# Last batch of an attention and expert layer: key sums and nine query transposes of a pair in one step, ten steps instead of twelve

## The chip, the cores and the metric

The kernel runs on one core of one Trainium2 chip. The metric is the device time of one execution in microseconds (us). Before the change it is 881.54 us, the median of three runs (880.99 to 881.73).

The core has five engines with a queue each, and each works its queue in order. PE does matrix products and transposes, and writes to PSUM (eight banks). ACT, DVE and POOL do element by element work; ACT and DVE read PSUM. SP issues most transfers.

## What is computed

Linear attention with random features for 4 batches of 8 heads (576 positions of 64 elements), then four experts on every position, each a product, a relu and a second product, weighted and summed:

```python
def phi(x):
    h = einsum('bhsd,md->bhsm', x, omega) - sum(x * x, -1) / 2
    return exp(h - max(h, -1)) / sqrt(m)
q_p, k_p = phi(q * D**-0.25), phi(k * D**-0.25)
kv, z = einsum('bhsm,bhsd->bhmd', k_p, v), sum(k_p, 2)
x = einsum('bhsm,bhmd->bhsd', q_p, kv) / (einsum('bhsm,bhm->bhs', q_p, z) + 1e-6)
...
for e in range(E):
    out += p[:, e:e + 1] * (relu(x @ w1[e]) @ w2[e])
```

The kernel splits an operand of a large product into a high and a low part of a faster number format (names that end in `h` and `l`) and adds three products, high by high, low by high and high by low.

## The kernel before, in words

The 2304 positions pass the experts in three blocks. Each block takes eight **visits**, one for half of the hidden units of an expert. The change concerns the second block, 768 positions, whose visits are numbered 1 to 8 here. They lie at 283.3, 316.0, 356.0, 392.7, 428.9, 466.6, 502.8 and 535.5 us of the profiled execution, and the last ends at 566.5 us.

While PE computes this block, the last batch's attention is worked in between. It has four **pairs** of heads, called pair 1 to 4 here. `later_ticks` (L469) is a generator that yields after each **step** of a pair, and `emit` (L1383) calls it at fixed points of the visits. Nothing reorders the work afterwards (`manual_schedule`), so every engine's queue is the order in which this code runs.

A visit is written by `fast` (L895). First come fourteen products of six matmuls each, seven for each of two groups of hidden units (`product`, L929; their matmuls are L937), and three half tiles of the second product (`begun`, L1006). Then come the rest of six output tiles (`outputs`, L751, its matmuls L756 to L758). A half tile is six matmuls. Where the first yield of a visit stands, after the products and the half tiles, is **slot 0**; slots 1 to 6 stand after output tiles 0 to 5. Slot 6 is the last before the next visit's products.

Four parts of a visit matter here:

- **Product 1 is copied before product 6.** Product 1 goes to a bank, ACT copies it to SBUF (`keep`, L941, its copy is L943), and product 6 adds to the same bank. Products 2 and 5 lie between. So PE reaches product 6 after eighteen matmuls, and waits there if the copy isn't done. Further on, the sums of `both` (L947, DVE, L951) free the banks of product 2 and 5.
- **The next visit's weights** are made in slices, one call of the generator `sides` (L675) after the products and after each output tile. After tile 1 DVE does four additions in place (L687 to L690) on the first half of the weights, after tile 2 ACT makes the high part (`w1sh`, L567) and POOL the low part (`w1sl`, L570). After tiles 3 and 4 the same comes for the second half. The additions write what the two others read.
- **The output tile** is weighted and added to `acc` by DVE (`gather`, L785), in visit 1 written by ACT (L783).
- **The stores of the weights** (`keep_sides`, L666) go over SP's queue ahead of later loads.

A pair's twelve steps, with the engines that they occupy:

1. keys projected on PE (L266, L277), their maxima on DVE (L282, L287), and the bias of the exponential on DVE (`bias`, L289: two small operations on 128 x 9 elements, L292 and L293, each with both inputs in SBUF)
2. the exponentials of the keys' tails and of the first half (ACT, L306 and L299), and the queries' squared lengths (DVE, L255)
3. the exponentials of the keys' second half (ACT, L299)
4. to 6. the same for the queries; steps 5 and 6 load the next pair's keys and queries
7. `sum_keys` (L309): eighteen matmuls on PE, evicted by ACT and DVE (L319, L320); the next pair's v is loaded and its keys are squared on POOL (L251)
8. `turn(0)` (L322): four transposes on PE, evicted by ACT and DVE (L338, L339)
9. `turn(1)`: five transposes (L328, L332), evicted likewise; the next pair's queries are squared on POOL
10. `numerators(0)` (L344): six matmuls, evicted by ACT (L365, L366); the next pair's lengths of the keys (L255, DVE)
11. `invert(0)` (DVE, L371), `times(0)` (POOL, L376), `numerators(1)`
12. `invert(1)`, `times(1)`

Six steps of `opening` (L378) come first: loads, squares on POOL and lengths of the first pair. That makes 54 steps.

How many steps a slot gets is set by a rate in `windows` (L1386): 54 steps over 0.8 of the 56 slots of the block, 1.205 a slot. After n slots all steps whose number is below 1.205 n have been written.

Of the kernel before, what the change touches and what calls it, by code (L numbers as in the profile page):

```python
# [14 lines left out]
def attention_moe(ctx, tc, kT, qT, kd, qd, kn, qn, vn, omT, probs, w1, w2, out):  # L15
# [11 lines left out]
    _, NP, D, _ = kT.shape  # L27
# [3 lines left out]
    E, FP, P, _ = w1.shape  # L31
# [69 lines left out]
    NV = len(HALVES)  # L101
# [276 lines left out]
    def opening(p, both=False):  # L378

        p.load("k")  # L380
        yield
        p.load("q")
        yield
        p.load_v()
        p.load_tails()
        yield
        p.square("k")
        yield
        p.square("q")
        yield  # L390
        p.lengths("k")
        if both:
            p.lengths("q")
        yield

    def joint_ticks(pairs):

        before = None
        for p, then in zip(pairs, pairs[1:] + [None]):
            p.project("k")  # L400
            p.project_tails("k")
            p.project("q")
            p.project_tails("q", beside="k")
            p.maxima("k")
            p.maxima_tails("k")
            p.bias("k")
            yield
            p.exp_tails("k")
            p.exp("k", 0)
            p.maxima("q")  # L410
            p.maxima_tails("q")
            p.bias("q")
            yield
            p.exp("k", 1)
            if then:
                then.load("k")
            yield
            if before:
                before.numerators(0)
            if then:  # L420
                then.load("q")
            yield
            p.exp_tails("q")
            p.exp("q", 0)
            if before:
                before.invert(0)
            if then:
                then.square("k")
            yield
            if before:  # L430
                before.numerators(1)
                before.times(0)
            if then:
                then.lengths("k")
                then.square("q")
            yield
            p.exp("q", 1)
            if before:
                before.invert(1)
            yield  # L440
            if before:
                before.times(1)
            if then:
                then.lengths("q")
            yield
            p.sum_keys()
            p.turn(0)
            p.turn(1)
            if then:
                then.load_v()  # L450
                if then.hp == 0:
                    then.load_tails()
            before = p
            yield
        yield from divided(before)
# [13 lines left out]
    def later_ticks(pairs):  # L469

        for p, then in zip(pairs, pairs[1:] + [None]):
            p.project("k")
            p.project_tails("k")
            p.maxima("k")
            p.maxima_tails("k")
            p.bias("k")
            yield
            p.exp_tails("k")
            p.exp("k", 0)
            p.lengths("q")  # L480
            yield
            p.exp("k", 1)
            yield
            p.project("q")
            p.project_tails("q")
            p.maxima("q")
            p.maxima_tails("q")
            p.bias("q")
            yield
            p.exp_tails("q")  # L490
            p.exp("q", 0)
            if then:
                then.load("k")
            yield
            p.exp("q", 1)
            if then:
                then.load("q")
            yield
            p.sum_keys()
            if then:  # L500
                then.load_v()
                then.square("k")
            yield
            p.turn(0)
            yield
            p.turn(1)
            if then:
                then.square("q")
            yield
            p.numerators(0)  # L510
            if then:
                then.lengths("k")
            yield
            p.invert(0)
            p.times(0)
            p.numerators(1)
            yield
            p.invert(1)
            p.times(1)
            yield  # L520
# [4 lines left out]
    BIG = {1: (START, 6 * P), 2: (START + 6 * P, 8 * P)}  # L525
# [5 lines left out]
    N0 = len(visits)  # L531
# [274 lines left out]
    def plain(v):  # L806
        n = visits[v][4]
        last = v == N0 - 1
        ready = sides(v + 1) if last else iter(())
        hs = []  # L810
        for f in range(FH):
            ps = bank("g1")
            hidden(v, f, n, ps, range(2))
            if n > 2 * P:
                yield 0.5
            hidden(v, f, n, ps, range(2, NP))
            hs.append(relu(ps, n))
            split_w()
            if f != 1:
                next(ready, None)  # L820
            if last and f:
                next(building, None)
            yield 0.5
        tiles = n // P
        for t in range(tiles):
            ps = bank("g2")
            outputs(v, hs, ps, t, range(2))
            if v == N0 - 2 and t in (0, 2):
                next(building)
            if last:  # L830
                next(building, None)
            yield 0.5
            outputs(v, hs, ps, t, range(2, FH))
            gather(v, ps, t)
            gathered(v, t)
            for _ in range(FH // tiles):
                split_w()
            next(ready, None)
            if last:
                next(building, None)  # L840
            yield 0.5
# [477 lines left out]
    def first_visit(g1):  # L1319
        hs = [relu(ps, 2 * P) for ps in g1[:2]]  # L1320
        yield 0.5
        for ps in g1[2:]:
            split_w(lo=nc.vector)
            hs.append(relu(ps, 2 * P))
            yield 0.5
        split_w(lo=nc.vector)
        split_w(lo=nc.vector)
        yield 0.5
        for t in range(2):
            ps = bank("g2")  # L1330
            outputs(0, hs, ps, t, range(FH))
            gather(0, ps, t)
            gathered(0, t)
            split_w()
            split_w(lo=nc.vector)
            yield 1

    def first_rest(pairs, then):

        def ahead(hp):  # L1340
            if hp < NP:
                pairs[hp].project("q", 1)
                pairs[hp].project("q", 2)

        def exps(hp):
            if hp < NP:
                pairs[hp].exp("q", 1)
                pairs[hp].exp("q", 2)

        ahead(0)  # L1350
        pairs[2].square("q1", nc.gpsimd)
        yield
        exps(0)
        ahead(1)
        pairs[3].square("q1", nc.gpsimd)
        yield
        for hp, p in enumerate(pairs):
            if hp:
                pairs[hp - 1].finish(1)
            p.turn(1, nc.vector)  # L1360
            p.turn(2, nc.vector)
            if hp == 0:
                nc.vector.tensor_scalar(om_r, om_r, QS, None, ALU.mult)
            if hp:
                next(then, None)
            yield
            exps(hp + 1)
            ahead(hp + 2)
            if hp:
                next(then, None)  # L1370
            yield
            p.numerators(1)
            yield
        pairs[-1].finish(1)
        yield

    def chain(*many):
        for x in many:
            yield from x
# [3 lines left out]
    def emit():  # L1383
        pairs, g1 = begin()
        later = [Halves(b, hp) for b in range(1, B) for hp in range(NP)]
        windows = {  # L1386
            0: (first_rest(pairs, opening(later[0], both=True)), 15 / 11),
            3: (joint_ticks(later[:-NP]), 76 / 45.4),
            N0: (chain(opening(later[-NP]), later_ticks(later[-NP:])), 54 / (NV * (BIG[1][1] // P + 1) * 0.8)),
        }  # L1390
        ticks, n, done, per = iter(()), 0, 0.0, 0
        for v in range(len(visits)):
            if v in windows:
                for _ in ticks:
                    pass
                ticks, per = windows[v]
                n, done = 0, 0.0
            for share in first_visit(g1) if v == 0 else fast(v) if v >= N0 else plain(v):
                done += share
                while n < done * per:  # L1400
                    next(ticks, None)
                    n += 1
        store(0)

    with tc.manual_schedule():
        emit()
# [58 lines left out]
```

## Time and profile before

| what | us |
|---|---|
| median of three runs | 881.54 |
| profiled execution | 883.9 |
| its span, first to last instruction | 882.1 |
| PE busy | 874.8 |
| DVE, POOL, ACT busy | 573.6, 553.1, 467.4 |

The profiled execution took 2.4 us longer than the median of the runs. PE has a matmul under way in 99% of the span, at the full granted clock in every slice of the page, so what the other engines do matters where PE has to wait for it. All times that follow are us from the start of the span. In a timeline a row is the start, the duration, the engine, the line, the operation and its tiles; an `x2` merges equal ones that follow each other; what stands in brackets is the engine's idle time before it and what ended that. Matmuls overlap, so their pace is read from their starts.

### The profile page before, as it was taken

To read this page: it belongs to the slowest core of one execution; us is meant where nothing else is said; L and a number is where in the kernel's file an instruction comes from. 1 tells how busy PE (TensorE), PEld (TensorE's weight loads), DVE (VectorE), ACT (ScalarE), POOL (GpSimd) and SP (SyncE) were. 2 spreads that over 40 slices of the span, in tenths; PEclk is the share of its full clock that TensorE was granted. 3 is DMA by queue.
4 is the path that set the end of the run, shared out by engine and by line. 5 is a ranking of instruction groups with operands and counts; after the bars stand their busy time and mean duration, and the time that the engine had idled before them with its cause. 6 is when DMAs were issued, how large, how long until landed. Compare 5 with 4: busy or idle time off the path is not lost.

```text
span 882.1 us, 14766 instructions
## 1 busy us (share of the span) xinstructions
PE 874.8 (99%) x5484; PEld 787.5 (89%) x5484; DVE 573.6 (65%) x1025; ACT 467.4 (53%) x1039; POOL 553.1 (63%) x494
## 2 busy tenths in 40 slices
PE   9999999999999989999999999999999999999998
PEld 9888898989888988989889899899989898998988
DVE  6755566666667556575756756965748476574847
ACT  6564687776774554556545554544443434444342
POOL 6656465555644454354444446779898887979874
PEclk9999999999999999999999999999999999999999
DMA  7565355444521847446274354645152442415132
GB/s 183 167 214 170 111 162 177 129 137 138 186 63 58 286 125 276 174 148 246 74 279 164 123 215 164 235 152 158 57 179 81 141 161 85 156 60 180 53 116 96
DMA packets 64296, 134.01 MB, mean 152 GB/s; under 512 B 10368, under 2 KB 20800, under 8 KB 64224
## 3 DMA queue, kind: packets, MB, share of 16 engines
q1 hardware_dynamic: 54256, 102.95, 35.9%
q0 software_dynamic: 9360, 29.82, 10.4%
q8 instruction: 43, 0.70, 0.3%
q10 hardware_dynamic: 608, 0.30, 0.1%
q14 instruction: 29, 0.24, 0.1%
HBM read 98.96 MB, written 34.08 MB: 151 GB/s over the span
## 4 chain that ended last, share of the span: by engine, by line
PE 97%; DVE 2%; DMA 1%; ACT 0%; issue 0%; POOL 0%; SPq 0%; POOLq 0%
PE g L937 30%; PE g L1015 18%; PE g L756 8%; PE g L758 8%; PE g L757 8%; PE g L741 3%; PE g L742 3%; PE g L743 3%; PE kv L317 2%; PE k_ps L266 1%; PE q_ps L266 1%; PE qt_ps L328 1%; PE k_ps L147 1%; PE kv L177 1%; PE nd L207 1%; PE nd L358 1%
## 5 line engine op out<-in xcount | busy, mean ns | idle before, releaser
L785 DVE SCALAR_TENSOR_TENSOR acc<-g,pr,acc 128x256 f32<-128x256 f32 (+1 forms) x278 | 140.2, 542 | 41.6 <-PE g L758 26.1
L570 POOL TENSOR_TENSOR w2l<-w2r,w2h 128x512 fp32r<-128x512 f32 x61 | 79.3, 1308 | 78.7 <-ACT w2h L567 67.3
L570 POOL TENSOR_TENSOR w1sl<-w1r,w1sh 128x512 fp32r<-128x512 f32 (+1 forms) x43 | 75.2, 1749 | 65.2 <-ACT w1sh L567 59.7
L756 PE MATMUL g<-w2h,hh 128*128 128x512 f32 x280 | 111.7, 399 | 0.0
L758 PE MATMUL g<-w2h,hl 128*128 128x512 f32 x280 | 109.6, 391 | 0.0
L757 PE MATMUL g<-w2l,hh 128*128 128x512 f32 x280 | 109.5, 391 | 0.0
L937 PE MATMUL g<-xbh,w1sh 128*128 128x384 f32 (+1 forms) x256 | 93.1, 364 | 2.3 <-ACT sum L943 2.3
L937 PE MATMUL g<-xbl,w1sh 128*128 128x384 f32 (+1 forms) x256 | 92.9, 363 | 0.0
L937 PE MATMUL g<-xbh,w1sl 128*128 128x384 f32 (+1 forms) x256 | 92.6, 362 | 0.0
L943 ACT ACTIVATE sum<-g 128x384 f32<-128x384 f32 (+1 forms) x96 | 52.2, 544 | 69.6 <-PE g L937 68.8
L570 POOL TENSOR_TENSOR w1al<-w1r,w1ah 128x512 fp32r<-128x512 f32 (+1 forms) x45 | 49.6, 1118 | 57.5 <-ACT w1ah L567 51.9
L937 PE MATMUL g<-xbh,w1ah 128*128 128x384 f32 (+1 forms) x192 | 69.9, 364 | 0.0
L937 PE MATMUL g<-xbl,w1ah 128*128 128x384 f32 (+1 forms) x192 | 69.6, 362 | 0.0
L937 PE MATMUL g<-xbh,w1al 128*128 128x384 f32 (+1 forms) x192 | 69.5, 362 | 0.0
L951 DVE TENSOR_TENSOR sum<-g,sum 128x384 f32<-128x384 f32 (+1 forms) x64 | 37.4, 588 | 44.3 <-PE g L937 38.7
L758 PEld LDWEIGHTS g<-w2h,hl 128*128 128x128 f32 x280 | 52.5, 188 | 11.4
L756 PEld LDWEIGHTS g<-w2h,hh 128*128 128x128 f32 x280 | 52.7, 188 | 10.1
L757 PEld LDWEIGHTS g<-w2l,hh 128*128 128x128 f32 x280 | 52.6, 188 | 9.0
L937 PEld LDWEIGHTS g<-xbh,w1sh 128*128 128x128 f32 x256 | 48.1, 188 | 8.3 <-ACT sum L943 2.6
L937 PEld LDWEIGHTS g<-xbl,w1sh 128*128 128x128 f32 x256 | 48.1, 188 | 5.2
L937 PEld LDWEIGHTS g<-xbh,w1sl 128*128 128x128 f32 x256 | 48.1, 188 | 5.1
L961 ACT ACTIVATE hh<-sum 128x384 fp32r<-128x384 f32 x48 | 25.1, 525 | 50.8 <-DVE sum L951 50.4
(220 smaller groups left out, 2472.2 us busy)
## 6 DMA issues: line engine op xcount, KB each, us to landing
w1r<-in_w SPq DMA_DIRECT2D x54, 512.0 KB, 3.7
w2r<-in_w SPq DMA_DIRECT2D x76, 256.0 KB, 3.1
kept<-w1sh SPq DMA_DIRECT2D x16, 512.0 KB, 5.3
kept<-w1sl SPq DMA_DIRECT2D x16, 512.0 KB, 5.5
w1sh<-kept POOLq DMA_DIRECT2D x16, 512.0 KB, 4.9
w1sl<-kept POOLq DMA_DIRECT2D x16, 512.0 KB, 5.6
kept<-w1ah SPq DMA_DIRECT2D x16, 384.0 KB, 4.9
kept<-w1al SPq DMA_DIRECT2D x16, 384.0 KB, 5.0
```

The costliest lines, as they stand in the source:

```text
L570: lo.tensor_tensor(c, t, f32(a), ALU.subtract)
L741: nc.tensor.matmul(ps[:, :n], a[:, w], hi, start=(hp == 0), stop=False)
L742: nc.tensor.matmul(ps[:, :n], a[:, w], lo, start=False, stop=False)
L743: nc.tensor.matmul(ps[:, :n], r[:, w], hi, start=False, stop=(hp == NP - 1))
L756: nc.tensor.matmul(ps, ha[:, ts_], wa, start=(c == 0), stop=False)
L757: nc.tensor.matmul(ps, ha[:, ts_], wc, start=False, stop=False)
L758: nc.tensor.matmul(ps, hc[:, ts_], wa, start=False, stop=(c == FH - 1))
L785: nc.vector.scalar_tensor_tensor(to, ps, sc, to, ALU.mult, ALU.add)
L937: nc.tensor.matmul(ps, a[:, w], x[:, k], start=(start and k + at == 0), stop=(k == 1 and at == 2), skip_group_check=not start)
L943: nc.scalar.activation(t, P_[g][where], AF.Copy)
L951: nc.vector.tensor_tensor(t, P_[g][where], kept, ALU.add)
L1015: nc.tensor.matmul(to, x, w, start=(start and f + k == 0), stop=(f + k == 3), skip_group_check=not start)
```

## The change

Step 7 now holds `sum_keys`, `turn(0)` and `turn(1)`: eighteen matmuls and nine transposes, with all their evictions, and the load and the square that step 7 had. The old step 8 is gone. What step 9 had besides, the square of the next pair's queries, goes to the front of `numerators(0)`. A pair has ten steps, the stage 46, and the rate is 46 over the same slots, 1.027 a slot.

```diff
             p.sum_keys()
+            p.turn(0)
+            p.turn(1)
             if then:
                 then.load_v()
                 then.square("k")
             yield
-            p.turn(0)
-            yield
-            p.turn(1)
             if then:
                 then.square("q")
-            yield
             p.numerators(0)
...
-            N0: (chain(opening(later[-NP]), later_ticks(later[-NP:])), 54 / (NV * (BIG[1][1] // P + 1) * 0.8)),
+            N0: (chain(opening(later[-NP]), later_ticks(later[-NP:])), 46 / (NV * (BIG[1][1] // P + 1) * 0.8)),
```

With the rate, other steps move too. Before, about every fifth slot got two steps; now nearly every slot gets one. Counted out from the two rates, the slots that the prediction speaks of (K for keys, Q for queries; project, first and second exponentials as E1 and E2):

| visit, slots | before | now |
|---|---|---|
| 1, slots 4, 5, 6 | pair 1: lengths and K project; K E1; K E2 | lengths; K project; K E1 |
| 2, slots 3, 4, 5, 6 | turn(0); turn(1); numerators(0); numerators(1) | Q E2; sum and turns; numerators(0); numerators(1) |
| 3, slots 3, 4, 5, 6 | pair 2: Q project; Q E1; Q E2 and sum; turn(0) | K E2; Q project; Q E1; Q E2 |
| 4, slots 0, 1, 2, 3 | pair 2: turn(1); numerators(0); numerators(1); invert(1) and, of pair 3, K project | sum and turns; numerators(0); numerators(1); invert(1) |
| 4, slots 4, 5, 6 | pair 3: K E1; K E2; Q project | K project; K E1; K E2 |
| 5, slot 6 | pair 3: invert(1), and K project of pair 4 | invert(1) |
| 6, slot 2 | pair 4: Q project | K E2 and Q project |

The number of instructions stays the same on every engine. From line 510 on, lines of the changed kernel are two lower (L943 is L941 there).

PE in visit 2 after output tile 3 (`kv` is pair 1's key sum, `qt_ps` its transposed queries, `g` the output tile), before:

```order
L313 MATMUL kv<-vb,kp 128x256
L317 MATMUL kv<-va,kp 128x128 x8
L756 MATMUL g_4137<-w2h,hh 128x512
L757 MATMUL g_4137<-w2l,hh 128x512
L758 MATMUL g_4137<-w2h,hl 128x512
L756 MATMUL g_4137<-w2h,hh 128x512
L757 MATMUL g_4137<-w2l,hh 128x512
L758 MATMUL g_4137<-w2h,hl 128x512
L328 MATMUL qt_ps<-ident,qp 128x128 x4
```

and now:

```order
L313 MATMUL kv<-vb,kp 128x256
L317 MATMUL kv<-va,kp 128x128 x8
L328 MATMUL qt_ps<-ident,qp 128x128 x8
L332 MATMUL qt_ps<-ident,qp 128x128
L754 MATMUL g_4222<-w2h,hh 128x512
L755 MATMUL g_4222<-w2l,hh 128x512
```

The transposes now follow the key sums with no matmul of a tile between them.

ACT at the end of visit 1 (`acc` an output tile, `kp` the exponentials of pair 1's keys, `sum` the copy of product 1 of visit 2), before:

```order
L567 ACTIVATE w1sh<-w1r 128x1024
L306 ACTIVATE kp<-t_ps,nbk 64x128 x2
L299 ACTIVATE kp<-k_ps,nbk 128x128 x4
L783 ACTIVATE acc<-g_3925,pr 128x512
L299 ACTIVATE kp<-k_ps,nbk 128x128 x4
L943 ACTIVATE sum<-g_3953 128x384
```

and now:

```order
L565 ACTIVATE w1sh<-w1r 128x1024
L781 ACTIVATE acc<-g_3915,pr 128x512
L306 ACTIVATE kp<-t_ps,nbk 64x128 x2
L299 ACTIVATE kp<-k_ps,nbk 128x128 x4
L941 ACTIVATE sum<-g_3948 128x384
```

Between the bias and the copy, ACT now has six exponentials instead of ten and no output tile.

ACT at the end of visit 3 (`qp` the exponentials of pair 2's queries, `sum` the copy of product 1 of visit 4), before:

```order
L306 ACTIVATE qp<-t_ps,nbq 64x128 x2
L299 ACTIVATE qp<-q_ps,nbq 128x128 x4
L567 ACTIVATE w1sh<-w1r 128x1024
L299 ACTIVATE qp<-q_ps,nbq 128x128 x4
L319 ACTIVATE kvh<-kv 128x256
L338 ACTIVATE qth<-qt_ps 128x512
L943 ACTIVATE sum<-g_4746 128x384
```

and now:

```order
L565 ACTIVATE w1sh<-w1r 128x1024
L306 ACTIVATE qp<-t_ps,nbq 64x128 x2
L299 ACTIVATE qp<-q_ps,nbq 128x128 x8
L941 ACTIVATE sum<-g_4721 128x384
```

All ten exponentials now stand between the second high part `w1sh` and the copy. At the end of visit 4 ACT's rows read the same with `kp` and `nbk`, for pair 3's keys.

DVE in visit 3 (`mxq`, `nbq`: maxima and bias of pair 2's queries), before:

```order
L785 SCALAR_TENSOR_TENSOR acc<-g_4537,pr,acc 128x512
L282 TENSOR_REDUCE mxq<-q_ps 128x4 x2
L287 TENSOR_REDUCE mxq<-t_ps 64x1 x2
L292 SCALAR_TENSOR_TENSOR mxq<-sqq,mxq 128x9
L293 SCALAR_TENSOR_TENSOR nbq<-sqq,mxq 128x9
L785 SCALAR_TENSOR_TENSOR acc<-g_4642,pr,acc 128x512
L687 TENSOR_TENSOR w1r<-w1r 128x256
L688 TENSOR_TENSOR w1r<-w1r 128x256
L689 TENSOR_TENSOR w1r<-w1r 128x256
L690 TENSOR_TENSOR w1r<-w1r 128x256
```

and now:

```order
L783 SCALAR_TENSOR_TENSOR acc<-g_4537,pr,acc 128x512
L783 SCALAR_TENSOR_TENSOR acc<-g_4620,pr,acc 128x512
L685 TENSOR_TENSOR w1r<-w1r 128x256
L686 TENSOR_TENSOR w1r<-w1r 128x256
L687 TENSOR_TENSOR w1r<-w1r 128x256
L688 TENSOR_TENSOR w1r<-w1r 128x256
L282 TENSOR_REDUCE mxq<-q_ps 128x4 x2
L287 TENSOR_REDUCE mxq<-t_ps 64x1 x2
L292 SCALAR_TENSOR_TENSOR mxq<-sqq,mxq 128x9
L293 SCALAR_TENSOR_TENSOR nbq<-sqq,mxq 128x9
```

The bias, which stood ahead of the second four additions, now stands behind them. In visit 4 it does so too, for pair 3's keys.

## Rows read from the trace of the kernel before

**Rows 1.** Waits of PE: who waited for whom, us in total, times, longest.

```profile
PE g L937 <- ACT sum L943: 2.3, 1, 2.3
```

**Rows 2.** Timeline of PE, start of visit 2: products 1, 5 (end) and 6.

```profile
316.01 0.33 PE L937 MATMUL g<-xbh,w1ah 128*128 128x384 f32 x1
...
318.99 0.34 PE L937 MATMUL g<-xbh,w1sl 128*128 128x384 f32 x1
321.61 0.44 PE L937 MATMUL g<-xbh,w1sh 128*128 128x384 f32 x1 [2.29 <-ACT sum L943]
```

**Rows 3.** Timelines of DVE, POOL and ACT around that wait.

```profile
311.83 0.76 DVE L255 TENSOR_REDUCE sqk<-k 128x9 f32<-128x576 f32 x1 [2.37 <-POOL k L251]
...
314.33 0.95 DVE L292 SCALAR_TENSOR_TENSOR mxk<-sqk,mxk 128x9 f32<-128x9 f32 x1
315.32 2.32 DVE L293 SCALAR_TENSOR_TENSOR nbk<-sqk,mxk 128x9 f32<-128x9 f32 x1
...
314.11 1.15 POOL L251 TENSOR_TENSOR q<-q 128x576 f32<-128x576 f32 x1
315.22 2.40 POOL L570 TENSOR_TENSOR w1sl<-w1r,w1sh 128x1024 fp32r<-128x1024 f32 x1
...
317.67 0.74 ACT L306 ACTIVATE kp<-t_ps,nbk 64x128 f32<-64x128 f32 x2 [2.54 <-DVE nbk L293]
...
321.01 0.55 ACT L943 ACTIVATE sum<-g 128x384 f32<-128x384 f32 x1
```

**Rows 4.** Timeline of PE, visit 5: second product 5 and the matmul before it.

```profile
436.18 0.34 PE L937 MATMUL g<-xbh,w1sl 128*128 128x384 f32 x1
436.49 0.44 PE L937 MATMUL g<-xbh,w1sh 128*128 128x384 f32 x1
```

**Rows 5.** Timeline of PE in an earlier stage, where the three already stand together.

```profile
97.09 0.59 PE L313 MATMUL kv<-vb,kp 128*128 128x256 f32 x2
...
99.30 1.04 PE L328 MATMUL qt_ps<-ident,qp 128*128 128x128 f32 x8
...
100.20 0.48 PE L756 MATMUL g<-w2h,hh 128*128 128x512 f32 x1
```

**Rows 6.** Timelines of DVE, ACT and POOL in visit 3.

```profile
383.09 0.42 DVE L690 TENSOR_TENSOR w1r<-w1r 128x256 f32<-128x256 f32 x1
...
384.10 1.28 DVE L282 TENSOR_REDUCE mxq<-q_ps 128x4 f32<-128x512 f32 x2
...
385.93 1.23 DVE L292 SCALAR_TENSOR_TENSOR mxq<-sqq,mxq 128x9 f32<-128x9 f32 x1
387.19 0.17 DVE L293 SCALAR_TENSOR_TENSOR nbq<-sqq,mxq 128x9 f32<-128x9 f32 x1
...
380.58 2.18 ACT L299 ACTIVATE kp<-k_ps,nbk 128x128 f32<-128x128 f32 x8
383.60 1.06 ACT L567 ACTIVATE w1sh<-w1r 128x1024 fp32r<-128x1024 f32 x1 [0.84 <-issue]
...
384.74 2.39 POOL L570 TENSOR_TENSOR w1sl<-w1r,w1sh 128x1024 fp32r<-128x1024 f32 x1 [5.05 <-ACT w1sh L567]
```

**Rows 7.** Timelines of DVE and POOL in visit 2: an addition under a square.

```profile
349.29 1.07 DVE L687 TENSOR_TENSOR w1r<-w1r 128x256 f32<-128x256 f32 x1
...
348.93 1.15 POOL L251 TENSOR_TENSOR q<-q 128x576 f32<-128x576 f32 x1
```

**Rows 8.** Timeline of PE: a projection, first matmul of visits 4 and 5.

```profile
380.49 1.16 PE L266 MATMUL q_ps<-om_r,q 64*128 64x128 f32 x16
...
392.72 0.42 PE L937 MATMUL g<-xbh,w1ah 128*128 128x384 f32 x1
...
428.94 0.44 PE L937 MATMUL g<-xbh,w1ah 128*128 128x384 f32 x1
```

**Rows 9.** Timelines of DVE and POOL: an inversion, the products behind another one.

```profile
356.02 1.74 DVE L371 RECIPROCAL dn<-dn 128x256 f32<-128x256 f32 x1
...
420.04 0.88 POOL L376 TENSOR_TENSOR raw_x<-nu,dn 128x64 f32<-128x64 f32 x2 [3.54 <-DVE dn L371]
```

## The prediction

> **What bounds the kernel now.** The page comes first: PE is busy for 874.8 of 882.1 us. A change that neither adds nor removes a matmul can move the end only by what PE waits, so the second view is PE's waits. In the block that the change touches they name one, 2.3 us [rows 1]. The third view is PE's own timeline, read for starts that lie too far apart. Within a product they stand 0.173 us apart. At 318.99 the next start is 2.62 us away instead of 0.17, and the one after it comes 0.1 late as well [rows 2]. Twice more a start is 0.31 us away, with 0.1 behind it, at 436.18 [rows 4] and likewise at 473.87: 0.24 and 0.25 us, too short for the list of waits. That is 3 us in a stage of 283 us, and it bounds what removing waits can bring; what new waits can cost has no such bound.
>
> **Where the first wait comes from.** Product 6 of visit 2 waits for ACT's copy of product 1, and ACT has ten exponentials ahead of it that wait for pair 1's bias. The bias is late because of DVE's two small operations. L293 is 0.17 us long where POOL is idle [rows 6], but took 2.32 us here and ended at 317.64, with POOL's low part (315.22 to 317.62). L292 took 0.95 us and ended with POOL's square (314.11 to 315.26) [rows 3]. In visit 2 an addition of 0.42 us likewise took 1.07 and ended 0.3 us after POOL's square of 348.93 to 350.08 [rows 7]. So, in these rows, a DVE operation with both inputs in SBUF doesn't run while POOL has one; the maxima, which read PSUM, do. The Trainium skill says the same (SBUF — State Buffer, "Who interferes with whom"): such a DVE instruction and a GpSimd instruction that reads SBUF take turns on a shared port, a whole instruction at a time. The trace agrees with 2.32 us for L293.
>
> **Joining the step, by itself.** In the earlier stage that already works so, the key sums take 2.21 us and the nine transposes 0.90 until the next tile starts, whose first matmul is 0.09 longer than the usual 0.39 [rows 5]. That is 9 times 0.11, the pace of transposes in a row, so leaving such a run is nearly free. Two runs fewer for each of four pairs save at most 0.1 us each, 0.8 us if the whole entry were saved, and 0 by these rows; I take 0. The evictions are the same instructions on ACT and DVE. They lie beside tiles, and `numerators(0)` is the one that could notice. In visit 2 PE reaches it at 351.75 by my count of the rows before it and its third matmul, the first that reads `qtl`, at 352.0. DVE has the second additions ahead of that eviction, held by a low part and by the square that step 7 brings to POOL, and is done at about 351.9. I put 0 to 0.3 us there, and take 0.1. In the other three visits the numbers leave 0.4 us or more.
>
> **What the new rate moves.** This is what counts.
>
> First wait, visit 2: **1.6 us gained.** Pair 1's projection comes one tile later, but its lengths (311.83) and POOL's queue, which the late transfer sets, stay. The maxima then end at 314.7, L292 is again held by the square, L293 by the low part, and the bias is ready at 317.65 as before. From there ACT has two tails (0.75) and four exponentials (0.25 each, by the eight of [rows 6]) instead of eight, and no output tile: the copy starts at 319.44 instead of 321.01, and PE follows 0.60 after its start, at 320.04 instead of 321.61. PE would be there at 319.0, so 1.0 us of the wait stays.
>
> Short waits, visits 5 and 6: **0.5 us gained.** Before, a projection stood in slot 6 of visits 4 and 5. Its four banks were full all through the products, until ACT came to them in slot 0, and the second product 5 waited for a bank. Now slot 6 has no projection at all.
>
> Product 6 of visit 4: **1.75 us lost.** Pair 2's queries are now projected in slot 4 of visit 3, with all ten exponentials in slots 5 and 6, right ahead of the copy. This is the pattern of visit 1 before. What the bias waits for follows from four sizes. From the end of the additions (383.51) ACT's high part and POOL's low part take until 387.13: 3.6 us, and POOL starts after 1.2 [rows 6]. The maxima take 1.8 (384.10 to 385.93), so the bias is issued while the low part runs, as 385.93 shows: L292 took 1.23 and ended with it. So the bias comes 3.8 us after the second additions. Tails 0.75, eight exponentials 2.0 and the copy 0.6 until PE (the first wait's 0.60) make 3.4: product 6 can start 7.2 us after the second additions. When do those end? The first ones end at 382.4: 383.5 before, less 0.7 each for a tile and the lengths that now come later, plus 0.2 since the keys' bias comes later. Their low part runs from 383.6 to 386.0. DVE comes to the second additions at 384.3, is held until 386.0, and needs 0.3 and three times 0.45: 387.7. Product 6 at 394.9. PE wants it at 393.2: visit 4 started at 392.72 [rows 8], now without 2.2 of key sums and 0.4 of transposes, and product 6 comes 18 matmuls (3.1 us, as from 316.01 to 319.16 in [rows 2]) later. That is 1.65, and 0.1 for starting again.
>
> Product 6 of visit 5: **2.3 us lost.** Pair 3's keys do the same in visit 4. The first additions end at 421.1. Their low part stands on POOL behind `times(0)`, which waits for an inversion of 1.74 us on DVE and takes 0.9 [rows 9]: it runs from 423.75 to 426.15. The second additions start then and alternate with `times(1)` (0.9): 428.5 if that holds an addition as the square did, 427.8 if not. No row shows an addition under L376; L251, its nearest kin, holds one [rows 7], so I take 428.3. Product 6 at 435.5. PE wants it at 433.3: 428.94 [rows 8], less 1.3 for a projection (1.16 and four tails) that is now in the next visit, plus 2.2 and 0.4 for sums and transposes that were in the last, plus 3.1. That is 2.2 (1.7 to 2.4) and 0.1. By the rule cited above the products of `times(1)` hold an addition too, which is the upper end, 2.4.
>
> In visit 6 the queries' projection and the second exponentials share slot 2, and one bank is freed by ACT about when PE wants it: 0 to 0.3, I take 0.1.
>
> **Sum.** -1.6 - 0.5 + 1.75 + 2.3 + 0.1 + 0.1 = +2.1 us: 884.2 for the profiled span of 882.1. The profiled execution (883.9) is 2.4 above the median; the waits don't depend on that, so the median goes from 881.54 to 883.6. I write 883.5. A measurement of this kernel tells about 0.2%, 1.76 us, from no change, so this is just beyond it.
>
> **Rivals.**
> - Only one of the two new waits comes, most likely visit 5's. The hold on visit 3's bias decides: if ACT's second high part starts 0.6 us later than counted against DVE, L293 slips in ahead of POOL, and product 6 is on time. 883.6 - 1.75 = 881.8, no change. For it: one operation more on ACT's queue would do. Against: all four sizes are from one visit's rows. Chance 0.24.
> - Faster: the bias isn't held in either visit, and only the gains stay: 881.54 - 2.1 + 0.2 = 879.6. Against it stand three held operations in [rows 3, 6]. It decides at the same point, L293 ahead of the second low part, twice. Chance 0.11.
> - Slower still: the waits add to what follows. A tile's weighting now stands behind the held bias on DVE, and banks come free later; or `numerators(0)` in visit 2 waits for longer than 0.3. Another 1.5 us, one low part less what lies beside it: 885.1. Chance 0.13.
> - The forecast has 0.52, between 882.9 and 884.5.
>
> **How the numbers follow.** The forecast is slower by over 0.2% (above 883.30) in two thirds of its cases. Slower: 0.35 + 0.13 = 0.48. Within: 0.17 + 0.24 = 0.41. Faster: 0.11. The range leaves out the faster case and the end of the slow one: 881.2 to 885.2.
>
> **What would show it.** PE's waits for the copy would be three instead of one: at about 1.0 in visit 2, 1.6 in visit 4 and 2.2 in visit 5, each `g` <- ACT `sum`. L293 in visits 3 and 4 would take far over 0.17 us and end with a POOL low part. The 0.31 us steps in the second product 5 of visits 5 and 6 would be gone. No wait on PE in visits 4 and 5 would refute the third and fourth terms; a wait in visit 2 that is still above 2 the first; any wait at the joined step itself, or at the first `numerators(0)` beyond 0.3, the claim that joining is free.

## The result, and the profile after

The changed kernel takes 886.06 us, the median of six executions (885.34 to 887.98), against 881.50 us for the kernel before in the same session (880.99 to 882.00). The ratio is 1.0053, with a 95% interval of 1.0040 to 1.0066: slower by 4.6 us. The forecast was slower too, but at 883.5 us, and its range ended at 885.2.

The profiled execution took 886.17 us with a span of 884.4. So this one is like its timed executions, which the one of before (883.9) was not. The page of after has PE as busy as before:

```profile
PE 875.6 (99%) x5484; PEld 788.2 (89%) x5484; DVE 577.0 (65%) x1025; ACT 467.3 (53%) x1039; POOL 552.8 (63%) x494
```

PE's waits, who waited for whom with the total in us, the times and the longest, answer to [rows 1] (L937 is L935 now, L943 is L941):

```profile
PE g L935 <- ACT sum L941: 3.6, 3, 1.6
...
PE g L935 <- ACT kp L306: 0.2, 1, 0.2
```

One wait for the copy of product 1 has become three, as the prediction said. PE's own timeline places them. These rows answer to [rows 2, 4], in visits 2, 4 and 5, and the last two are the queries' projection of visit 6 and the next tile:

```profile
319.06 0.34 PE L935 MATMUL g<-xbh,w1sl 128*128 128x384 f32 x1
319.78 0.44 PE L935 MATMUL g<-xbh,w1sh 128*128 128x384 f32 x1 [0.38 <-ACT sum L941]
...
391.27 0.34 PE L935 MATMUL g<-xbh,w1sl 128*128 128x384 f32 x1
393.16 0.44 PE L935 MATMUL g<-xbh,w1sh 128*128 128x384 f32 x1 [1.55 <-ACT sum L941]
...
429.45 0.34 PE L935 MATMUL g<-xbh,w1al 128*128 128x384 f32 x1
429.95 0.44 PE L935 MATMUL g<-xbh,w1sh 128*128 128x384 f32 x1 [0.16 <-ACT kp L306]
...
430.93 0.34 PE L935 MATMUL g<-xbh,w1sl 128*128 128x384 f32 x1
432.92 0.44 PE L935 MATMUL g<-xbh,w1sh 128*128 128x384 f32 x1 [1.64 <-ACT sum L941]
...
490.41 1.59 PE L266 MATMUL q_ps<-om_r,q 64*128 64x128 f32 x15
...
492.27 0.50 PE L754 MATMUL g<-w2h,hh 128*128 128x512 f32 x1
```

Starts that lie 0.173 us apart elsewhere are 0.72, 1.89, 0.50 and 1.99 apart here, and about 0.1 follows each. The projection takes 1.86 us from its start to the tile's, where 381.41 to 382.72 us in visit 3 shows the usual 1.31: 0.55 lost.

The next fence has the timelines of DVE, POOL and ACT behind these three waits, in the order of visits 2, 4 and 5, each with the small operation of the bias, the low part and the copy; they answer to [rows 3, 6]:

```profile
314.95 2.26 DVE L292 SCALAR_TENSOR_TENSOR mxk<-sqk,mxk 128x9 f32<-128x9 f32 x1
...
314.78 2.40 POOL L568 TENSOR_TENSOR w1sl<-w1r,w1sh 128x1024 fp32r<-128x1024 f32 x1
...
319.22 0.51 ACT L941 ACTIVATE sum<-g 128x384 f32<-128x384 f32 x1
...
382.48 1.99 DVE L685 TENSOR_TENSOR w1r<-w1r 128x256 f32<-128x256 f32 x1
...
387.59 1.89 DVE L292 SCALAR_TENSOR_TENSOR mxq<-sqq,mxq 128x9 f32<-128x9 f32 x1
...
381.80 2.39 POOL L568 TENSOR_TENSOR w1sl<-w1r,w1sh 128x1024 fp32r<-128x1024 f32 x1 [3.94 <-ACT w1sh L565]
387.06 2.39 POOL L568 TENSOR_TENSOR w1sl<-w1r,w1sh 128x1024 fp32r<-128x1024 f32 x1 [2.88 <-ACT w1sh L565]
...
392.56 0.54 ACT L941 ACTIVATE sum<-g 128x384 f32<-128x384 f32 x1
...
427.36 1.89 DVE L292 SCALAR_TENSOR_TENSOR mxk<-sqk,mxk 128x9 f32<-128x9 f32 x1
...
426.83 2.39 POOL L568 TENSOR_TENSOR w1sl<-w1r,w1sh 128x1024 fp32r<-128x1024 f32 x1 [2.42 <-PE g L755]
...
432.32 0.54 ACT L941 ACTIVATE sum<-g 128x384 f32<-128x384 f32 x1
```

Each L292 ends within 0.04 us of the low part beside it, and takes 1.89 to 2.26 us for work that takes 0.17 at 340.02 us of this execution, where POOL is idle. The first of the second additions (382.48) is held by the first low part in the same way: it takes 1.99 us instead of 0.42 and ends 0.28 behind it. In visits 4 and 5 this is the chain of the prediction. In visit 2 it is L292 that the low part holds, where the prediction had L292 held by the square and L293 by the low part.

So the mechanism is there, near its predicted size, and still the time is 2.5 us off. Where those went was the first question.

### The profile page after: what moved, and what is told of

It reads as the page before. It is cut to its first block, busy times and chain, and to the rows that moved or that the text cites. A ratio compares the mean times of both kernels' runs of the same rounds, so it can differ in the third digit from the quotient of the medians.

```text
span 884.4 us, 14756 instructions
## 1 busy us (share of the span) xinstructions
PE 875.6 (99%) x5484; PEld 788.2 (89%) x5484; DVE 577.0 (65%) x1025; ACT 467.3 (53%) x1039; POOL 552.8 (63%) x494
## 4 chain that ended last, share of the span: by engine, by line
PE 92%; DVE 5%; ACT 1%; issue 1%; DMA 0%; POOL 0%; ACTq 0%; POOLq 0%
PE g L935 30%; PE g L1013 18%; PE g L754 7%; PE g L755 7%; PE g L756 7%; PE g L739 3%; PE g L740 3%; PE g L741 3%; PE kv L317 2%; PE k_ps L266 1%; PE q_ps L266 1%; PE qt_ps L328 1%; PE kv L177 1%; PE nd L358 1%; PE nd L356 1%
## 5 line engine op out<-in xcount | busy, mean ns | idle before, releaser
L935 PE MATMUL g<-xbh,w1sh 128*128 128x384 f32 (+1 forms) x256 | 93.2, 364 | 3.7 <-ACT sum L941 3.6
L935 PE MATMUL g<-xbl,w1sh 128*128 128x384 f32 (+1 forms) x256 | 92.9, 363 | 0.0
L935 PE MATMUL g<-xbh,w1sl 128*128 128x384 f32 (+1 forms) x256 | 92.6, 362 | 0.0
L941 ACT ACTIVATE sum<-g 128x384 f32<-128x384 f32 (+1 forms) x96 | 52.3, 545 | 65.9 <-PE g L935 65.0
L935 PE MATMUL g<-xbh,w1ah 128*128 128x384 f32 (+1 forms) x192 | 69.6, 362 | 0.0
L935 PE MATMUL g<-xbl,w1ah 128*128 128x384 f32 (+1 forms) x192 | 69.6, 362 | 0.0
L935 PE MATMUL g<-xbh,w1al 128*128 128x384 f32 (+1 forms) x192 | 69.5, 362 | 0.0
L949 DVE TENSOR_TENSOR sum<-g,sum 128x384 f32<-128x384 f32 (+1 forms) x64 | 37.4, 587 | 45.5 <-PE g L935 39.8
L935 PEld LDWEIGHTS g<-xbh,w1sh 128*128 128x128 f32 x256 | 48.1, 188 | 10.2 <-ACT sum L941 4.5
L935 PEld LDWEIGHTS g<-xbl,w1sh 128*128 128x128 f32 x256 | 48.1, 188 | 5.2
L935 PEld LDWEIGHTS g<-xbh,w1sl 128*128 128x128 f32 x256 | 48.1, 188 | 5.1
L965 DVE SCALAR_TENSOR_TENSOR hl<-sum,hh 128x384 fp32r<-128x384 f32 x48 | 27.8, 583 | 37.5 <-ACT hh L959 36.8
```

What stands on the lines that cost most here:

```text
L935: nc.tensor.matmul(ps, a[:, w], x[:, k], start=(start and k + at == 0), stop=(k == 1 and at == 2), skip_group_check=not start)
L941: nc.scalar.activation(t, P_[g][where], AF.Copy)
L949: nc.vector.tensor_tensor(t, P_[g][where], kept, ALU.add)
L965: nc.vector.scalar_tensor_tensor(x, y, 0.0, f32(z), ALU.max, ALU.subtract)
```

## The experiments

Each kernel was timed against the kernel before in the same session; the medians of before lay between 881.2 and 881.4 us there.

**The kernel before, again.** No edit.

> The kernel before, once more, for a second profile. The question is where the 2.4 us lay by which its first profiled execution was longer than its timed runs. My theory: in the wait of product 6 of visit 2, which the late transfer of the keys sets, so that a typical run doesn't have the gain of 1.6 us that I credited. Then a profiled execution near 881.5 us (span near 879.8) shows that wait under 0.7 us instead of 2.3, and the stage of the change is about 1.6 to 2.4 us shorter than 283.2 us. Rival: the wait belongs to the kernel and stays at 2.0 us or more in a profile of 881.5 us; the 2.4 us then lie outside the stage or spread over it. The timed median is 881.5 us by both.

881.54 us in median; the profiled execution took 881.11, with a span of 879.3. PE's waits, of the whole kernel, are these two, both ahead of the stage:

```profile
PE warm L1191 <- DVE om_r L1182: 1.1, 1, 1.1
PE k_ps L147 <- POOL k L140: 0.2, 1, 0.2
```

The wait of visit 2 is gone. The timelines of DVE, POOL and ACT at the place of [rows 3] show why:

```profile
313.33 0.96 DVE L292 SCALAR_TENSOR_TENSOR mxk<-sqk,mxk 128x9 f32<-128x9 f32 x1
314.32 0.17 DVE L293 SCALAR_TENSOR_TENSOR nbk<-sqk,mxk 128x9 f32<-128x9 f32 x1
...
309.65 1.15 POOL L251 TENSOR_TENSOR k<-k 128x576 f32<-128x576 f32 x1 [2.26 <-DMA k<-in_kn]
...
313.11 1.16 POOL L251 TENSOR_TENSOR q<-q 128x576 f32<-128x576 f32 x1
314.98 2.40 POOL L570 TENSOR_TENSOR w1sl<-w1r,w1sh 128x1024 fp32r<-128x1024 f32 x1 [0.72 <-ACT w1sh L567]
...
318.12 0.55 ACT L943 ACTIVATE sum<-g 128x384 f32<-128x384 f32 x1
```

The rows of the keys came earlier: POOL's square starts at 309.65 instead of 310.65, which is 0.78 us earlier against the start of visit 2. L293 then falls into the 0.72 us in which POOL waits for ACT's high part, and takes 0.17 us instead of 2.32. The copy starts at 318.12 instead of 321.01. Visit 2 is 2.58 us shorter, and all other visits are the same within 0.04; the stage is 2.54 us shorter than the 283.20 us of the first profile. So the wait is a race that the chain loses or wins with the arrival of one transfer, and the execution that the prediction read had lost it. By their times most executions win: of the 66 of the kernel before that were timed beside the other kernels in these sessions, 57 lie below 882.0 us and six at 883.8 or above. Of the eleven of this run ten lie below 882.0, and one took 883.76.

**The changed kernel, again.** No edit.

> The changed kernel, once more, for a second profile. By both theories the waits of product 6 in visits 4 and 5 are there again, 1.4 to 1.8 us each, and the time is 886.0 us. If the late transfer is a matter of chance in each execution, the wait in visit 2 (0.4 us in its first profile) varies between 0 and 0.7 us, and the start of the kernel by some tenths of a us.

885.93 us, ratio 1.0053 (1.0041 to 1.0065). The waits in visits 4 and 5 come again with 1.88 and 1.97 us between starts. In visit 2 the square on the rows of the keys also started earlier than in the first profile (by 0.55 us, or 0.20 against the start of the visit), but here that changes little: L292 was held again and took 2.04 us, and PE's step is 0.49 instead of 0.72.

**The joined step in the old slots.**

```diff
 p.sum_keys()
+p.turn(0)
+p.turn(1)
 if then:
     then.load_v()
     then.square("k")
 yield
-p.turn(0)
 yield
-p.turn(1)
 if then:
     then.square("q")
```

> The key sums and both runs of transposes in one step as in the change, but at the old rate of 54 steps, with an empty step in the place of each transposing one, so that every other step stays in its old slot. My claim is that joining costs nothing by itself: 881.5 us (880.7 to 881.8), no wait on PE at the joined step, and the waits of PE as in the kernel before. Rival: the joined step itself is what the 4.5 us are for, through banks or evictions: 883 us or more, with waits right after the transposes or at the numerators.

884.51 us, ratio 1.0045 (1.0028 to 1.0061). The claim fell here. PE's waits name the transposes:

```profile
PE qt_ps L328 <- ACT qp L299: 2.0, 3, 1.3
```

The timelines of PE and ACT at the joined step of visit 3, where the longest of them is:

```profile
387.10 0.38 PE L328 MATMUL qt_ps<-ident,qp 128*128 128x128 f32 x2
388.83 1.10 PE L328 MATMUL qt_ps<-ident,qp 128*128 128x128 f32 x6 [1.35 <-ACT qp L299]
...
388.43 1.12 ACT L299 ACTIVATE qp<-q_ps,nbq 128x128 f32<-128x128 f32 x4
```

In the old slots the second exponentials of pair 2's queries are issued in the same slot as the key sums, and ACT has a high part of the weights ahead of them; of pair 4's (visit 6, the other two waits of the list) both exponentials share the slot before. Pairs 1 and 3 share a slot in the same way as pair 2, and there no transpose waits. The key sums don't read these exponentials, the transposes do. So joining is free only where the second exponentials are done in time. The change's ten steps put a tile between, and there eight of the nine transposes stand in a row without a wait, as PE's timeline of visit 2 of the changed kernel shows:

```profile
346.09 1.04 PE L328 MATMUL qt_ps<-ident,qp 128*128 128x128 f32 x8
```

**The maxima in PSUM.** In the changed kernel a pair's maxima go to free columns of the bank of its tails, so that L292 and L293 read one input from SBUF instead of two:

```diff
 p.project_tails("k")
+p.mxk = p.t_psk[0][:, M:M + 9]
-p.maxima("k")
 p.maxima_tails("k")
+p.maxima("k")
 p.bias("k")
```

and likewise for the queries.

> The changed kernel, with the maxima of a pair's rows kept in free columns of the bank of its tails in PSUM, so that both small operations of the bias read one input from SBUF instead of two. Theory (a DVE operation with both inputs in SBUF doesn't run while POOL has one): the first small operation falls from 1.9 us in visits 3 and 4 to under 0.4 us while POOL's low part runs, the exponentials start 1.6 us or so earlier, the waits of product 6 in visits 4 and 5 (1.55 and 1.64 us) shrink to 0.2 us or less, and the time falls by 2.8 to 3.8 us, to 882.2 to 883.2 us. Rival: the small operations end with POOL's low part for another reason; then they still take 1.5 us or more, and the time stays at 885.5 to 886.5 us.

882.84 us, ratio 1.0014 (1.0005 to 1.0023): 3.1 us of the 4.6 are gone, which the theory said. PE's waits for the copy:

```profile
PE g L937 <- ACT sum L943: 1.1, 2, 0.7
```

The timelines of DVE and POOL in visit 3:

```profile
381.74 1.99 DVE L687 TENSOR_TENSOR w1r<-w1r 128x256 f32<-128x256 f32 x1
...
387.22 0.17 DVE L292 SCALAR_TENSOR_TENSOR t_ps<-sqq,t_ps 128x9 f32<-128x9 f32 x1
...
386.32 2.40 POOL L570 TENSOR_TENSOR w1sl<-w1r,w1sh 128x1024 fp32r<-128x1024 f32 x1 [2.88 <-ACT w1sh L567]
```

L292 takes 0.17 us in the middle of the low part that held it for 1.89. The addition, which still reads SBUF twice, still takes 1.99, and the waits of visits 4 and 5 shrink without vanishing: by the products of these visits, 17.88 and 18.19 us instead of 19.04 and 19.58, where 17.20 is the length without any wait. The expected 0.2 us or less was too good. The held additions are enough for the rest in visit 4 (1.6 us lost there on the way to the bias), but not in visit 5, where they lose only 0.7 of the 0.9 us by which PE's step is too long; no run takes this hold away. The maxima that write PSUM cost DVE 0.26 us more for each projection (1.44 and 0.70 us instead of 1.28 and 0.60), and the first numerators of visit 2 waited for 0.2 us here.

**The steps one slot earlier.** In the changed kernel the lengths of the first pair's keys share a step with their projection:

```diff
         if both:
             p.lengths("q")
-        yield
+            yield
...
-            N0: (chain(opening(later[-NP]), later_ticks(later[-NP:])), 46 / (NV * (BIG[1][1] // P + 1) * 0.8)),
+            N0: (chain(opening(later[-NP]), later_ticks(later[-NP:])), 45 / (NV * (BIG[1][1] // P + 1) * 0.8)),
```

> The changed kernel, with the lengths of the first pair's keys in the same step as its keys' projection: 45 steps at 45 over the same slots, and every later step one slot earlier. Both of the new waits of 1.6 us come, by my theory, from projections that fall into slot 4 with all exponentials in slots 5 and 6; now they stand in slot 3 (visits 3 and 4), as in the kernel before, and the first pair's keys in slot 4 of visit 1, as there. Theory: 881.2 to 882.0 us, no wait of product 6 in visits 4 and 5, and now and then 2.4 us in visit 2 as in the kernel before. Rival: the joined step or the ten steps cost by themselves, wherever they stand: 883.5 us or more, with waits at the joined step (transposes on the second exponentials, one tile behind them) or at the first numerators.

Counted out from the rate, every step from the first pair's projection of its keys to the last pair's second exponentials of its keys stands one slot earlier. What follows stays in its slot, so these exponentials no longer share slot 2 of visit 6 with the projection of the queries.

881.34 us, ratio 0.9993 (0.9979 to 1.0008); one of the twelve executions took 885.38. The joined step is there, the ten steps are there, and no loss can be told from the noise. PE's waits in the profile:

```profile
PE warm L1189 <- DVE om_r L1180: 1.1, 1, 1.1
PE k_ps L266 <- DMA k<-in_kd: 1.0, 1, 1.0
```

The second is a transfer of this execution that came late, ahead of visit 2. No product waits. So what the change costs is where its new rate puts the projections.

**The same, with the maxima in PSUM.** The edits of the last two kernels together.

> The same as open5, and besides the maxima in PSUM as in psum_max. Theory: 880.9 to 881.6 us, without the occasional wait in visit 2, as no small operation of a bias waits for POOL any more; against the kernel before at most 0.5 us faster, since all that PE waits there in a typical execution of this stage is under 1 us. Rival as for open5: 883 us or more.

881.17 us, ratio 0.9991 (0.9980 to 1.0003), and all twelve executions within 880.58 to 882.09. By the medians it is 4.9 us shorter than the changed kernel. Against the kernel before the interval includes 1, so it can't be called faster.

**The rows of the keys later, in the kernel before.** First by two transfers (the order of the transfers on SP's queue, not the code; `kn` and `qn` are the rows):

```diff
 load("k"):  k <- kd
-            k <- kn
 load("q"):  q <- qd
             q <- qn
+            k <- kn
```

> The kernel before, with one transfer of the first pair (the rows of its keys, for their lengths) issued behind the two of its queries instead of ahead of them, about 1.1 us later on SP's queue. Theory: the wait in visit 2 is a race between the bias and the low part that POOL starts 0.7 us behind a square: with the rows 1.0 us later the second small operation of the bias misses the gap in every execution, takes 2.3 us instead of 0.17, and the time is 883.4 to 884.4 us, with a wait of 2.0 us or more in each. Rival: one transfer later by 1 us moves nothing, 881.0 to 881.7 us, and the long executions of the kernel before have another cause.

886.67 us, ratio 1.0050 (1.0032 to 1.0068): both were wrong. The square on the rows started 2.2 us later than in the second profile of the kernel before (1.9 against the start of visit 2), not 1.1. The timelines of POOL and DVE:

```profile
311.89 1.15 POOL L255 TENSOR_TENSOR k<-k 128x576 f32<-128x576 f32 x1 [4.21 <-DMA k<-in_kn]
...
316.57 2.31 DVE L297 SCALAR_TENSOR_TENSOR nbk<-sqk,mxk 128x9 f32<-128x9 f32 x1
```

PE's wait for the copy:

```profile
PE g L943 <- ACT sum L949: 3.4, 1, 3.4
```

And the stretches behind it: length, busy time of PE, PEld, DVE, ACT and POOL with the number of instructions, PE's granted clock, DMA share, GB/s:

```profile
323.00:325.00 2.00, 2.00 (x7) 2.00 (x8) 0.38 (x1) 1.21 (x3) 1.61 (x2) 0.50 0.04 8
325.00:327.00 2.00, 2.00 (x10) 2.00 (x9) 0.00 (x0) 0.63 (x2) 0.91 (x1) 0.66 0.51 133
327.00:330.00 3.00, 3.00 (x19) 3.00 (x18) 2.11 (x4) 1.81 (x5) 0.00 (x0) 1.00 0.33 86
```

L297 (L293 there) is held as expected. But the products of visit 2 take 22.43 us instead of 17.20, and the step to product 6 is 3.73 us long where 0.17 is usual: 3.6 of these 5.2. The rest is a second effect: behind PE's 3.4 us of idleness its granted clock is at 0.50, the level of 1.2 GHz, and the products' matmuls start 0.32 us apart instead of 0.173.

Then by one transfer, so that the wait stays short:

```diff
 load("k"):  k <- kd
-            k <- kn
 load("q"):  q <- qd
+            k <- kn
             q <- qn
```

> The kernel before, with the rows of the first pair's keys issued behind one transfer of its queries instead of two as in kn_late: about 0.6 us later on SP's queue than in the kernel before. In kn_late the rows came 2.2 us later than usual and PE idled for 3.4 us, after which its granted clock was at half for some 3 us. Theory: here the bias again misses the gap ahead of the low part in most executions, but the wait stays near 2.5 us and the clock at full: 883.4 to 884.6 us. Rival: the rows come early enough for the gap, 881.0 to 881.8 us; or the cost of kn_late is of another kind and comes in full, 885.5 us or more.

884.45 us, ratio 1.0036 (1.0023 to 1.0048): the theory's case. PE's wait for the copy:

```profile
PE g L941 <- ACT sum L947: 2.3, 1, 2.3
```

The timelines of DVE and POOL ahead of it:

```profile
315.17 2.31 DVE L297 SCALAR_TENSOR_TENSOR nbk<-sqk,mxk 128x9 f32<-128x9 f32 x1
...
315.06 2.39 POOL L574 TENSOR_TENSOR w1sl<-w1r,w1sh 128x1024 fp32r<-128x1024 f32 x1
```

These are [rows 1, 3] over again, and the clock stays at 1.00. The lowest of its eight executions is 883.71 us. The square starts at 310.49, 0.84 us later than in the second profile of before (0.79 against the start of visit 2). So the rows issued one transfer later make the first profile of before the rule.

**The late rows, with the maxima in PSUM.** The edits of kn_late and psum_max in the kernel before.

> The kernel before with the late transfer of kn_late and the maxima in PSUM as in psum_max. Theory: without two inputs in SBUF the bias no longer misses a gap, so the late transfer costs nothing: 881.0 to 881.7 us, no wait of product 6 in visit 2. Rival: the late transfer delays the chain by itself, beyond the bias: 882.5 us or more.

882.67 us, ratio 1.0010 (0.9998 to 1.0022): 4.0 less than kn_late, and still in the rival's range. DVE's timeline has the counterpart of L293, and PE's waits the copy:

```profile
315.98 0.17 DVE L297 SCALAR_TENSOR_TENSOR nbk<-sqk,t_ps 128x9 f32<-128x9 f32 x1
...
PE g L945 <- ACT sum L951: 0.9, 1, 0.9
```

The bias is no longer held, as the theory said, but the late transfer delays the chain by itself, as the rival said: visit 2 is 38.68 us long instead of 37.44, 1.2 us more.

**Visit 6 without the shared slot.** In the changed kernel the rate is 45.5 instead of 46; until visit 6 no step moves.

> The changed kernel at 45.5 instead of 46 steps over the same slots. Until visit 6 every step stays in its slot; there the last pair's second exponentials of the keys and projection of its queries no longer share slot 2, the projection comes one slot later, and so do the steps behind it. Theory: the projection's wait for a bank goes (it took 0.55 and 0.7 us more than elsewhere in the two profiles), and nothing else changes: 885.2 to 885.6 us, with 16 matmuls of the projection in 1.16 us and the waits of product 6 in visits 4 and 5 as before. Rival: the same wait is put into another place, 885.8 to 886.2 us.

885.24 us, ratio 1.0041 (1.0025 to 1.0057). The interval overlaps that of the changed kernel, so it is the profile that separates the two. The projection of the queries in visit 6 takes its usual time:

```profile
491.26 1.16 PE L266 MATMUL q_ps<-om_r,q 64*128 64x128 f32 x16
```

Visits 6 and 7 together are 0.54 and 0.67 us shorter than in the changed kernel's two profiles, and the waits of visits 4 and 5 stay (steps of 1.88 and 1.98 us). So the projection that shares slot 2 with the second exponentials of the keys is a term of its own, as is told below.

## Why the prediction missed, point by point

The terms are measured by the length of a visit's fourteen products, from the start of their first matmul to that of their last with two half tiles between (17.20 us without a wait), and, for visit 6, by the projection as well. The first column of results compares the two profiles that were shown first, the second the two further ones, in which before is a typical execution.

| term | forecast, us | first profiles | second profiles |
|---|---|---|---|
| wait in visit 2 | -1.6 | 19.77 to 17.87: -1.90 | 17.20 to 17.65: +0.45 |
| product 6 of visit 4 | +1.75 | 17.28 to 19.04: +1.76 | 17.28 to 19.02: +1.74 |
| visit 5, short wait gone, product 6 | -0.25 + 2.3 | 17.57 to 19.58: +2.01 | 17.58 to 19.55: +1.97 |
| short wait in visit 6 | -0.25 | 17.58 to 17.20: -0.38 | 17.58 to 17.20: -0.38 |
| projection in visit 6 | +0.1 | +0.55 | +0.70 |
| numerators(0) in visit 2 | +0.1 | 0 | 0 |
| sum | +2.15 | +2.04 | +4.48 |
| the whole block | | +2.04 | +4.39 |

- **The step that failed** is the last one, from the profiled execution to the median: "The profiled execution (883.9) is 2.4 above the median; the waits don't depend on that". The wait of [rows 1] was itself that excess. The typical execution has no wait in visit 2 to shorten, so 1.6 us were credited that only the profiled execution could give back, and 0.45 of a new one was missed: 2.05 of the 2.3 us between the forecast sum and that of the second profiles. Most of the rest is the projection in visit 6. The prediction had both numbers side by side, 2.4 us of excess and a wait of 2.45 that begins at a late transfer, and three timed executions within 0.74 us of each other, so that either all of them had the wait or none. The second profile shows that it was none: without the wait it took 881.11 us.
- **The mechanism behind that wait** was read rightly, and even its dependence on the late transfer was written down; what wasn't asked is how far L293 was from the gap. It started 0.10 us after POOL's low part in [rows 3], and POOL had to wait for neither ACT nor anything else. kn_mid shows that the arrival of these rows decides it.
- **In visit 2 of the changed kernel** some wait stays, as was said (1.0), but less: PE's step is 0.55 and 0.32 us longer than the usual 0.17. The maxima read PE's projection a slot later, and L292 met the low part in each of the three profiles with these slots (2.26, 2.04 and, in rate455, 2.08 us).
- **Product 6 of visits 4 and 5**, the two largest terms, came within 0.1 us of the forecast. psum_max shows the hold to be what is said of it, a DVE operation with two SBUF inputs standing still while POOL's low part runs: with one input moved to PSUM L292 took 0.17 us instead of 1.89. The Trainium skill (SBUF — State Buffer, "Who interferes with whom") says that a DVE instruction with at most one SBUF input, outside the 2-port modes, does not contend with GpSimd. The 0.17 us of L292 under the low part agree. open5 shows the slots to be the cause: with the same joined step one slot earlier both waits are gone. In visit 5 a part of the loss is another wait, of product 5 at 429.95 for ACT's tails (0.50 us instead of 0.17, and 0.1 behind it: 0.4). It was not foreseen, but it changes no sum: product 6 starts when the copy is there, so what PE waits at product 5 is missing from the wait of product 6, which was 0.4 shorter than forecast (1.99 less 0.17, and 0.1: 1.9). From the end of the second additions to product 6 it was 7.3 us in both visits, where the forecast had 7.2. Whether `times(1)` holds an addition, which the prediction left open, these rows of DVE and POOL settle:

```profile
423.70 0.99 DVE L686 TENSOR_TENSOR w1r<-w1r 128x256 f32<-128x256 f32 x1
...
423.34 1.06 POOL L376 TENSOR_TENSOR raw_x<-nu,dn 128x320 f32<-128x320 f32 x1
```

  The addition took 0.99 us instead of 0.42 and ended 0.29 behind the product. The four were done 1.9 us before the visit, as in the forecast, which had taken a value between its two cases.
- **The projection in visit 6** was mis-sized: 0.55 to 0.70 us where 0 to 0.3 stood. rate455 takes the two steps apart, and the loss is gone.
- **Joining by itself** costs nothing in the change, but for a reason that the prediction didn't give. It looked at the matmuls and evictions alone; join_only shows that the transposes also need the second exponentials, and that in the old slots PE waits 2.0 us for them; the stage is 3.1 us longer there than in the second profile of before. The new rate puts these exponentials a tile earlier.
- **The rivals.** "Slower still" came nearest with its time (885.1) but not with its reason: by the table the waits added nothing to what follows, and the first numerators didn't wait. The two rivals with fewer waits are ruled out by L292, which was held in both visits.

What stays open: six of those 66 executions of the kernel before take 883.8 us or more, five of these over 885. That the five have a longer wait with a lowered clock behind it, as kn_late has, would fit: their mean granted clock is 0.997 or 0.998, as in kn_late's profiled execution (0.998), and that of the sixth (883.82 us) is 1.000. But no profile caught one, so where they wait is not shown.

## What to carry to other kernels

Before a wait of a profile is counted as a gain, hold the profiled execution against the timed ones: where it is longer by about that wait, and the wait begins at a transfer, profile the kernel a second time or cost the change without it. Where a small DVE operation stands on the way to PE, look how far it is from POOL's next long operation; one of its inputs in PSUM took the race out here, for 0.26 us more in the maxima. And a step that moves by one slot is costed by what it now stands beside, for each pair and each visit, since here the same joined step gave 881.3, 884.5 and 886.1 us in three sets of slots.

## What was not expected of the hardware

PE idle for 3.4 us in visit 2 of kn_late had its clock granted at 0.50 afterwards, and then 0.66 in the mean of the next 2 us, in which it rose from 1.2 to 2.4 GHz; that cost 1.7 us beside the wait (5.23 less 3.56). The waits of 1.6 to 2.3 us in the other kernels left it at 1.00. A wait that grows from 2.3 to 3.4 us therefore cost twice as much here: 5.2 us against 2.6.
